# Other SBUF places and another order of sums for the last rows of x in a layer-scale kernel

## The chip, the cores and the metric

The kernel runs on one core of one Trainium2 chip. The metric is the device time of one execution in microseconds (us); lower is better.

## The reference

`x` and `y` are [1024, 16, 512] in bf16, `gamma` is [512] in bf16. The result is elementwise, with `gamma` spread over the first two dimensions:

```python
def reference(x, y, gamma):
    return x + gamma * y
```

Flattened, there are 16,384 rows of 512 elements. Each of the three large tensors (x, y and the output) has 16.78 MB.

## The kernel before

The 16,384 rows are divided over the 128 partitions of SBUF: each partition holds 128 rows of 512 elements, 1 KB per row and partition. "Row r" below means row r of every partition, so one row stands for 128 KB of data. `BLOCKS = [4, 64, 60]` says how the rows lie in DRAM: rows 0 to 4, 4 to 68 and 68 to 128 are three blocks, and within a block the rows of one partition are contiguous. A transfer of rows 4 to 68 is therefore 128 contiguous stretches of 65,536 bytes, one for each partition; one of rows 68 to 128 is 128 stretches of 61,440 bytes, and one of rows 68 to 120 is 128 stretches of 53,248 bytes.

The whole of y stays in SBUF (`y_sb`, 128 rows). The product and the sum are both written over it, and the output is stored from it. For x there are only 76 places (`x_sb`, 76 rows), so that the last rows of x are loaded over rows that have already been used. The lists at the top of the file set everything:

- `SP` is the sequence of loads that SyncE (SP) issues. `('x', 68, 120, 16)` loads rows 68 to 120 of x into the places from 16 on. `ACT` is the sequence that ScalarE issues: gamma, then three stores, of rows 4 to 68, 0 to 4 and 68 to 128.
- `PIECES = [16, 52, 52, 8]` cuts the 128 rows into the pieces that VectorE works on: piece 0 is rows 0 to 16, piece 1 rows 16 to 68, piece 2 rows 68 to 120, piece 3 rows 120 to 128.
- `DVE` is VectorE's sequence. `('m', c)` multiplies piece c of y by gamma in place (L181), `('a', c)` adds x to it (L190).
- `HOLD` and `AHEAD`: SP waits before its third load until rows 0 to 4 of y are in.
- `RELEASE`: the stores wait until the load of rows 68 to 120 of x has landed. TensorE waits for it and then raises two semaphores, `s_go` for ScalarE (L159) and `s_rel` for VectorE (L160).

Ahead of each load of x, `frees(w)` finds the pieces whose sums read the places that the load will write over, and SP waits until that many sums are done (semaphore `s_add`, which every sum raises by one; L36 is the helper for other waits). SP's queue is in order: the wait ahead of one load also holds back those behind it. In the kernel before, the load of rows 68 to 120 goes over places 16 to 68, which piece 1 reads, and piece 1 is summed first; so SP waits for one sum, and then issues this load and the load of rows 120 to 128 (into places 68 to 76, which nothing used before) one directly after the other (L133).

gamma is spread over the partitions by one matmul with a row of ones (L153) and a copy out of PSUM (L155). At the end SP waits for all stores.

Of the kernel before, what the change touches and what calls it, by code (L numbers as in the profile page):

```python
# [5 lines left out]

BLOCKS = [4, 64, 60]

PIECES = [16, 52, 52, 8]


SP = [
# [2 lines left out]
    ('x', 0, 4, 0),  # L15
    ('x', 4, 68, 4),
    ('y', 68, 128),
    ('x', 68, 120, 16),
    ('x', 120, 128, 68),
]  # L20
ACT = [('g',), ('s', 4, 68), ('s', 0, 4), ('s', 68, 128)]

# [1 line left out]

HOLD, AHEAD = ('y', 0, 4), (2, 0)

RELEASE = ('x', 68, 120, 16)

DVE = [('m', 0), ('m', 1), ('a', 1), ('a', 0), ('m', 2), ('m', 3), ('a', 2), ('a', 3)]
MULT, ADD = mybir.AluOpType.mult, mybir.AluOpType.add  # L30


def _take(sem, n, eng):


    return eng.wait_ge(sem, n).then_inc(sem, -n)  # L36


def kernel(
# [18 lines left out]
    rows = N // P  # L58
    n = len(PIECES)
    assert sum(PIECES) == rows  # L60
    starts = [sum(PIECES[:c]) for c in range(n + 1)]
    dt = xf.dtype
# [27 lines left out]
    s_add, s_go, s_rel, s_end, s_out = sem("s_add"), sem("s_go"), sem("s_rel"), sem("s_end"), sem("s_out")  # L90
    added = [a for kind, *a in DVE if kind == "a"]
    order = {a[0]: k for k, a in enumerate(added)}

    def meets(a, b, c, d):
        return a < d and c < b
# [4 lines left out]
    def x_at(row):  # L100
        return next(w[3] + row - w[1] for w in x_loads if w[1] <= row < w[2])
# [55 lines left out]

    _take(s_load[RELEASE], 16, nc.tensor)
    nc.tensor.sem_inc(s_go, 1)  # L159
# [4 lines left out]
    def need(loads, c):  # L164
        for w in loads:
            if w not in landed and meets(starts[c], starts[c + 1], w[1], w[2]):
                if w == RELEASE:
                    _take(s_rel, 1, nc.vector)
                elif w == HOLD:
                    _take(s_held[nc.vector], 1, nc.vector)  # L170
                else:
                    _take(s_load[w], 16, nc.vector)
                landed.add(w)

    for kind, *args in DVE:
        c = args[0]
        yt = y_sb[:, starts[c] : starts[c + 1], :]
        if kind == "m":
            need(y_loads, c)
            g = gamma_sb[:, None, :].to_broadcast([P, PIECES[c], D])  # L180
            nc.vector.tensor_tensor(out=yt, in0=yt, in1=g, op=MULT).then_inc(s_dve, 1)  # L181
            open_mults += 1
        else:
# [4 lines left out]
            at = x_at(starts[c])  # L188
            xt = x_sb[:, at : at + PIECES[c], :]
            nc.vector.tensor_tensor(out=yt, in0=xt, in1=yt, op=ADD).then_inc(s_add, 1)  # L190
# [44 lines left out]
```

## Time and profile before

| | |
|---|---|
| time, median of 7 executions | 120.51 us (120.27 to 120.65) |
| time of the profiled execution | 120.31 us |
| its span in the trace | 119.0 us (118.99 before rounding) |
| moved by DMA | 50.33 MB, 423 GB/s over the span |
| VectorE busy | 69.9 us, 59% |
| TensorE (PE) busy | 0.6 us |

The span is the part of an execution that the trace covers; 1.32 us of the profiled time lie outside it. Times inside the trace count from the start of the span. "From issue to landing" is the time from the instruction that issues a transfer to the moment when all of it has arrived. Where the text speaks of windows, a row gives the window, its length, the busy time of each engine in it with the number of instructions, the TensorE clock, the busy time of the 16 DMA engines as a share of 16 engines over that window, and the rate. In that view a DMA engine's transfer of one stretch counts whole in the window in which it starts, so the share of a short window can be far above 1. From such a row follow the number of stretches that start in it (rate times length, divided by the bytes of a stretch) and their mean duration (share times 16 times length, divided by that number).

### The profile page before, as it was taken

What the parts mean: (1) busy time and instruction counts of PE and PEld (TensorE: products, weight loads), DVE (VectorE), ACT (ScalarE), POOL (GpSimd) and SP (SyncE); (2) the same over time, 40 slices, a digit from 0 to 9 for tenths busy, and PEclk for the clock granted to TensorE, in tenths of its full rate; (3) what the DMA queues carried; (4) which work ended last, traced back from release to release, by engine and by line L of the source; (5) the groups of instructions that cost most, each with busy time, mean ns of one, the idle gap of its engine ahead of it and who ended that gap; (6) DMA issues with size and microseconds to landing.
All of it is one profiled execution on the core that took longest, in us unless ns stands there. A gap on an engine that the chain in (4) does not pass through costs nothing. (4 is left out here: it accounts for less than half of the span.)

```text
span 119.0 us, 89 instructions
## 1 busy us (share of the span) xinstructions
PE 0.6 (0%) x1; PEld 0.1 (0%) x1; DVE 69.9 (59%) x10; POOL 0.2 (0%) x4
## 2 busy tenths in 40 slices
PE   0001000000000000000000000000000000000000
PEld 0000000000000000000000000000000000000000
DVE  0002000399999839999999999989999800000000
POOL 0000000000000000000000000000000000000000
DMA  9888998988898879779869797998898889798790
GB/s 529 352 353 352 529 529 352 529 352 352 352 683 375 352 330 661 330 330 640 351 286 555 304 555 304 386 606 352 352 683 375 352 352 507 330 640 351 330 640 21
DMA packets 1442, 50.33 MB, mean 423 GB/s; under 512 B 161, under 2 KB 162, under 8 KB 546
## 3 DMA queue, kind: packets, MB, share of 16 engines
q1 hardware_dynamic: 1008, 33.55, 65.8%
q10 hardware_dynamic: 434, 16.78, 32.7%
HBM read 33.56 MB, written 16.78 MB: 423 GB/s over the span
## 5 line engine op out<-in xcount | busy, mean ns | idle before, releaser
L181 DVE TENSOR_TENSOR y_sb<-y_sb,gamma_sb 128x26624 bf16<-128x26624 bf16 (+2 forms) x4 | 34.6, 8686 | 11.0 <-DVEq L36 11.0
L190 DVE TENSOR_TENSOR y_sb<-x_sb,y_sb 128x26624 bf16<-128x26624 bf16 (+2 forms) x4 | 34.6, 8688 | 2.8 <-DVEq L36 2.8
L155 DVE CAST gamma_sb<-gamma_ps 128x512 bf16<-128x512 f32 x1 | 0.7, 691 | 9.0 <-DVEq L36 9.0
L147 DVE MEMSET ones_row<- 1x128 bf16 x1 | 0.2, 165 | 2.0 <-PEq L52 2.0
L153 PE MATMUL gamma_ps<-gamma_row,ones_row 1*128 1x512 bf16 x1 | 0.6, 577 | 10.4 <-PEq L36 10.4
L153 PEld LDWEIGHTS gamma_ps<-gamma_row,ones_row 1*128 1x128 bf16 x1 | 0.1, 99 | 10.4 <-issue 10.4
L219 POOL MEMSET const-bfloat16-1.0<- 128x1 bf16 x1 | 0.1, 102 | 0.0
L219 POOL MEMSET const-uint8-127<- 128x1 uint8 x1 | 0.1, 102 | 0.0
L219 POOL MEMSET const-float32-1.0<- 128x1 f32 x1 | 0.1, 99 | 0.0
L219 POOL MEMSET const-float32-0.0<- 128x1 f32 x1 | 0.1, 98 | 0.2 <-issue 0.2
## 6 DMA issues: line engine op xcount, KB each, us to landing
y_sb<-in_y_dram SPq DMA_DIRECT2D x1, 7680.0 KB, 57.0
out_dram<-y_sb ACTq DMA_DIRECT2D x1, 7680.0 KB, 24.2
x_sb<-in_x_dram SPq DMA_DIRECT2D x1, 6656.0 KB, 20.2
x_sb<-in_x_dram SPq DMA_DIRECT2D x1, 1024.0 KB, 22.3
y_sb<-in_y_dram SPq DMA_DIRECT2D x1, 512.0 KB, 3.3
x_sb<-in_x_dram SPq DMA_DIRECT2D x1, 512.0 KB, 20.3
out_dram<-y_sb ACTq DMA_DIRECT2D x1, 512.0 KB, 22.3
y_sb<-in_y_dram SPq DMA_DIRECT2D x1, 22.3
```

The costliest lines, as they stand in the source:

```text
L147: nc.vector.memset(ones_row, 1.0).then_inc(s_ones, 1)
L153: nc.tensor.matmul(gamma_ps, ones_row, gamma_row, start=True, stop=True).then_inc(s_ps, 1)
L155: nc.vector.tensor_copy(out=gamma_sb, in_=gamma_ps).then_inc(s_dve, 1)
L181: nc.vector.tensor_tensor(out=yt, in0=yt, in1=g, op=MULT).then_inc(s_dve, 1)
L190: nc.vector.tensor_tensor(out=yt, in0=xt, in1=yt, op=ADD).then_inc(s_add, 1)
L219: nc = _bacc.Bacc("TRN2", target_bir_lowering=False, num_devices=1)
```

## The change

The lists at the top of the file change, the code below them does not. Rows 0 to 68 are cut into three pieces instead of two, so there are five pieces: rows 0 to 8, 8 to 24, 24 to 68, 68 to 120 and 120 to 128. The load of rows 68 to 120 of x goes into places 24 to 76 instead of 16 to 68, and the load of rows 120 to 128 into places 0 to 8 instead of 68 to 76; `x_sb` keeps its 76 places. VectorE first sums rows 24 to 68, then rows 0 to 8, then rows 8 to 24. What `frees` answers changes with it: the load of rows 68 to 120 waits for one sum, which is now that of 44 rows, and the load of rows 120 to 128 waits for a second sum, that of rows 0 to 8.

```diff
-PIECES = [16, 52, 52, 8]
+PIECES = [8, 16, 44, 52, 8]
...
     ('y', 68, 128),
-    ('x', 68, 120, 16),
-    ('x', 120, 128, 68),
+    ('x', 68, 120, 24),
+    ('x', 120, 128, 0),
 ]
...
-RELEASE = ('x', 68, 120, 16)
-
-DVE = [('m', 0), ('m', 1), ('a', 1), ('a', 0), ('m', 2), ('m', 3), ('a', 2), ('a', 3)]
+RELEASE = ('x', 68, 120, 24)
+
+DVE = [('m', 0), ('m', 1), ('m', 2), ('a', 2), ('a', 0), ('a', 1), ('m', 3), ('m', 4), ('a', 3), ('a', 4)]
```

The stores still need the sums of their own rows: three sums instead of two for rows 4 to 68, five instead of four for the last store. Their order and sizes, and those of the loads, stay as they are.

## Prediction

> **What bounds the kernel now.** I read the page's load lines first, then VectorE's timeline, the waits of SP's queue, the DMA issues, and last narrow windows around the moment at which one load hands over to the next.
>
> ```profile
> DMA  9888998988898879779869797998898889798790
> ...
> q1 hardware_dynamic: 1008, 33.55, 65.8%
> q10 hardware_dynamic: 434, 16.78, 32.7%
> HBM read 33.56 MB, written 16.78 MB: 423 GB/s over the span
> ```
>
> The DMA engines are busy from end to end. 50.33 MB at 423 GB/s is the whole span. A stretch of 61,440 bytes takes 2.267 us on one engine (last row of the window table below: 1.42 x 16 x 0.10), which is 27.1 GB/s, or 434 GB/s for sixteen; at that pace 50.33 MB take 116.1 us. The first transfer starts at 1.0 us, and SP sees the last landing about 0.37 us after it ends. So some 1.5 us of the 119.0 are left for everything else. VectorE, busy 69.9 us, is not the bound, as its timeline shows:
>
> ```profile
> 22.83 18.36 DVE L181 TENSOR_TENSOR y_sb<-y_sb,gamma_sb 128x8192 bf16<-128x8192 bf16 x2 [11.02 <-DVEq L36]
> 43.58 18.36 DVE L190 TENSOR_TENSOR y_sb<-x_sb,y_sb 128x26624 bf16<-128x26624 bf16 x2 [2.39 <-DVEq L36]
> 57.63 0.81 SPq L133 DMA_DIRECT2D x_sb<-in_x_dram  x2
> 61.85 16.22 DVE L181 TENSOR_TENSOR y_sb<-y_sb,gamma_sb 128x26624 bf16<-128x26624 bf16 x2
> 78.20 16.89 ACTq L139 DMA_DIRECT2D out_dram<-y_sb  x3
> 78.49 16.23 DVE L190 TENSOR_TENSOR y_sb<-x_sb,y_sb 128x26624 bf16<-128x26624 bf16 x2 [0.41 <-DVEq L36]
> ```
>
> VectorE waits 2.39 us for x before its first sum at 43.58. That sum ends at 57.60, and at 57.63 SP issues the two last loads. The next two lines say that SP had waited for that sum, and how long the loads took:
>
> ```profile
> SPq L133 <- DVE y_sb L190: 52.7, 1, 52.7
> ```
>
> ```profile
> y_sb<-in_y_dram SPq DMA_DIRECT2D x1, 7680.0 KB, 57.0
> ...
> x_sb<-in_x_dram SPq DMA_DIRECT2D x1, 6656.0 KB, 20.2
> x_sb<-in_x_dram SPq DMA_DIRECT2D x1, 1024.0 KB, 22.3
> ```
>
> The load of y's last 60 rows, issued at 4.50, lands 57.0 us later, at 61.5. So when SP issues x's next load at 57.63, the engines still have some 3 us of y to move. Seen this way the issue is not late, and the change would buy nothing. The windows around the handover say more:
>
> ```profile
> 42.50:42.60 0.10, 0.00 (x0) 0.00 (x0) 0.00 (x0) 0.00 (x0) 1.00 5.70 2458
> 60.66:60.73 0.07, 0.00 (x0) 0.00 (x0) 0.07 (x1) 0.00 (x0) 1.00 8.49 3043
> 60.73:61.20 0.47, 0.00 (x0) 0.00 (x0) 0.47 (x1) 0.00 (x0) 1.00 3.15 1360
> 62.65:63.15 0.50, 0.00 (x0) 0.00 (x0) 0.50 (x1) 0.00 (x0) 1.00 3.69 1597
> 63.15:63.70 0.55, 0.00 (x0) 0.00 (x0) 0.55 (x1) 0.00 (x0) 1.00 0.00 0
> 63.70:63.80 0.10, 0.00 (x0) 0.00 (x0) 0.10 (x1) 0.00 (x0) 1.00 1.23 532
> 115.60:116.00 0.40, 0.00 (x0) 0.00 (x0) 0.00 (x0) 0.00 (x0) 1.00 5.33 2304
> 116.00:116.30 0.30, 0.00 (x0) 0.00 (x0) 0.00 (x0) 0.00 (x0) 1.00 0.00 0
> 116.30:116.40 0.10, 0.00 (x0) 0.00 (x0) 0.00 (x0) 0.00 (x0) 1.00 1.42 614
> ```
>
> The first row is the handover from x's rows 4 to 68 to y's rows 68 to 128, whose load had been issued 38 us before. Four stretches start in it (2458 x 0.10 / 61,440 bytes), mean 2.28 us: the normal 2.267. The next two rows are the handover to the load issued at 57.63. The twelve engines that reach it after 60.73 need 1.97 us for 53,248 bytes, but the four that reach it before 60.73 need 2.38 us on average (8.49 x 16 x 0.07 / 4), together 1.6 us too long. The transfer records show where this lies: 3.02 us instead of 1.97 on one engine, 0.36 and 0.18 us too long on two others, nothing on any later one. The rows from 62.65 on show the result: fifteen engines start their second stretch by 63.15, none in the next 0.55 us, one at 63.75. An engine that was among the first four is now the last by 0.62 us. It never recovers, because every engine has the same bytes still to move: in the last three rows fifteen engines start their last stretch before 116.00, none for 0.3 us, and one at 116.35. That engine ends at 118.62, the one before it at 118.16. So the end of the span is one engine's delay of 1.05 us, of which 0.45 shows.
>
> That only the first to arrive were delayed is how it looks when something of the new load (its descriptors, or the first data) is not ready yet. The latest engine got going at about 60.73 + 1.05 = 61.78, that is 4.15 us after the issue.
>
> **The change part by part.**
>
> The sums that decide the issue. The groups by shape give VectorE's price per row:
>
> ```profile
> L190 DVE TENSOR_TENSOR y_sb<-x_sb,y_sb 128x26624 bf16<-128x26624 bf16 x2 | 28.1, 14026 | 2.8 <-DVEq L36 2.8
> L190 DVE TENSOR_TENSOR y_sb<-x_sb,y_sb 128x8192 bf16<-128x8192 bf16 x1 | 4.4, 4418 | 0.0
> L190 DVE TENSOR_TENSOR y_sb<-x_sb,y_sb 128x4096 bf16<-128x4096 bf16 x1 | 2.3, 2284 | 0.0
> ```
>
> From 4,096 to 26,624 elements is 11.74 us for 44 rows of 512. So the new sum of 44 rows costs 11.74 + 0.15 (what is left of the 2.28) = 11.89 us, against 14.03. It still starts at 43.58: the three products ahead of it take 2.28 + 4.42 + 11.89 = 18.59 us, against 18.44 for two, which ends by 41.4, inside the wait for x. Without that cover of 2.2 us the extra product would cost about 0.1. The sum ends at 55.47, so SP issues x's rows 68 to 120 at 55.49, 2.14 us sooner. The lead over the first engine's arrival at 60.69 grows from 3.06 to 5.20 us. The slowest engine needed 4.15, so 1.05 us are to spare, and its delay goes: -1.05 us on that engine. Late next is the engine that ends at 118.16: -0.45 us on the span.
>
> The load of rows 120 to 128. It gets a wait of its own, for the sum of rows 0 to 8, which ends 2.2 us later, at 57.7. It is issued at about 57.7 instead of 58.0. Nothing stands behind it in SP's queue but the final waits, and its bytes come after those of rows 68 to 120, from 76.4 on: the lead is 18.7 us. Cost: nothing; it would have to be some 14 us later to matter.
>
> The release. Rows 68 to 120 land at 57.63 + 20.2 = 77.85 now; without the late engine, 0.5 us sooner. The stores (78.20 in the timeline) follow 0.35 us behind that landing, so at 77.7. The loads of rows 120 to 128 keep the engines busy until 79.0 to 79.5, which covers that issue as it does now. Store and load may then overlap a little on an engine; the bytes are the same, and I put this at 0. By the trace, where stores start at 79.07 with 2.48 instead of 2.42 us on the engines that come first, its bounds are -0.1 and +0.1 us.
>
> VectorE afterwards. One product and one sum more, and each adds about 0.07 us to the pace of the chain (0.15 of fixed time, of which 0.08 overlaps the instruction before, as the starts in the timeline show: 14.03 + 4.42 = 18.45 for a line of 18.36). The products of the last 60 rows end at 78.14 instead of 78.07. The next sum starts at 78.49 now, held by the release; later by the products, at about 78.3. The last sum ends at 94.6 instead of 94.7. The last store's bytes have their turn at 99.76. Cost: nothing under a cover of 5 us; without it, 0.07 us.
>
> Here a rule of the Trainium skill speaks against the change. The page "DMA: Bandwidth & Descriptors", section "Latency and other measured facts", puts the first byte of a transfer issued from SP or ScalarE at about 0.6 us. By it a lead of 3.06 us hides the start five times over, the extra lead is worth 0.00 us, and the forecast would be 120.51. The row 60.66:60.73 disagrees for a queue whose engines are all busy: 4.15 us on the worst of sixteen. The trace's own cold start agrees with the rule more nearly (issued at 0.00, first stretch at 1.00). I go by the row, since it was measured at this very place. Its weakness is that it is one event in one execution.
>
> The sum: 118.99 - 0.45 = 118.54 us of span, 119.86 with the 1.32 outside it. The profiled execution (120.31) stands 0.20 below the median of 120.51; applied to the median, 120.51 - 0.45 = 120.06. Executions above the profiled one may have had a longer or more unfortunate delay, in which case they gain more.
>
> **The rivals.**
>
> Same: the delay isn't tied to the lead. It could be a chance event of that execution, or belong to the first reads of rows 68 to 120 wherever they are issued. For it: only one load in the trace is issued late, and 3 us ought to suffice by the rule. Against it: that the three that were hit are all among the first four of sixteen would be 1 in 140 by chance, and no early load shows it. Time 120.51, 120.4 to 120.6. That the change doesn't move the issue at all can nearly be excluded: SP's wait is for one sum, and that sum is shorter.
>
> Slower: the delay is made by issuing any load while the engines are in their last stretch of y (58.4 to 61.1), when the generation of its descriptors gets in the way of theirs. Rows 120 to 128 are still issued at 57.7, so the delay stays and may fall on another engine. The engines arrive from 60.69 to 61.17. An engine delayed by 1.05 us that arrives at p ends at 118.62 + (p - 60.73); for the last one that is +0.44 us, 120.95. It is slower by over 0.24 us from p = 60.97 on, which is five of sixteen engines. For it: in the last stretch of y most transfers take 10 to 30 ns more than 2.267 us, and 65 on one. Against it: in the trace the late engines were spared.
>
> **How the numbers follow.** The delay goes: 0.62, at 120.06. Its own range is 119.8 to 120.25: at best 0.7 us is gained, if the median's extra 0.20 is the same delay on a later engine (the free engines ending between 117.9 and 118.16 set the floor), at worst half of it remains. Same: 0.22, at 120.51. Slower: 0.16, at 120.95. A measurement of this kernel can tell 0.2% (0.24 us) from no change, and the first case lies beyond that. The range of 119.75 to 120.65 takes in the first two and the small end of the third, and leaves out about 0.15.
>
> **What would show it.** Right: SP issues rows 68 to 120 at about 55.5; the stretches that start first at the handover near 60.7 take 1.97 us like the later ones; no engine starts its second stretch alone after 63.2; sixteen engines start their last stretch within about 0.5 us; ScalarE's first store is issued near 77.7. Wrong: an engine with a first stretch of over 2.5 us is still there, or the last stretch still starts alone. In that case the time has not moved, or has grown.

## The result and the profile after

The changed kernel takes 119.78 us (median of 12 executions, 119.70 to 120.02), the kernel before 120.45 us (median of 31, 119.88 to 120.76). The ratio is 0.9951, with a 95% interval of 0.9940 to 0.9962: 0.5% faster, some 0.6 us. The profiled span is 118.42 us, against 118.99.

The page of the changed kernel shows the same picture as before, full DMA engines over the whole span, a little denser:

```profile
DMA  9888998988899879979969696898899889798792
...
HBM read 33.56 MB, written 16.78 MB: 425 GB/s over the span
```

The timeline shows SP's two last loads (the line of 55.57), the first stores (77.63) and VectorE's groups:

```profile
43.65 18.43 DVE L190 TENSOR_TENSOR y_sb<-x_sb,y_sb 128x22528 bf16<-128x22528 bf16 x3 [2.29 <-DVEq L36]
55.57 2.53 SPq L133 DMA_DIRECT2D x_sb<-in_x_dram  x2
62.00 16.22 DVE L181 TENSOR_TENSOR y_sb<-y_sb,gamma_sb 128x26624 bf16<-128x26624 bf16 x2
77.63 17.33 ACTq L139 DMA_DIRECT2D out_dram<-y_sb  x3
78.36 16.23 DVE L190 TENSOR_TENSOR y_sb<-x_sb,y_sb 128x26624 bf16<-128x26624 bf16 x2
```

SP issues rows 68 to 120 at 55.57, 2.06 us sooner than before. The second issue of that line is at 57.77. The DMA issues of the two loads, with the time to landing in the last column:

```profile
x_sb<-in_x_dram SPq DMA_DIRECT2D x1, 6656.0 KB, 21.7
x_sb<-in_x_dram SPq DMA_DIRECT2D x1, 1024.0 KB, 22.0
```

Rows 68 to 120 now need 21.7 us instead of 20.2, so of 2.06 us of earlier issue 1.5 are spent waiting in the queue, and the landing is 0.56 us sooner (77.28 instead of 77.85). What the earlier issue brings is seen in the windows, read as in the prediction:

```profile
60.55:60.73 0.18, 0.00 (x0) 0.00 (x0) 0.18 (x1) 0.00 (x0) 1.00 4.80 2071
60.73:61.20 0.47, 0.00 (x0) 0.00 (x0) 0.47 (x1) 0.00 (x0) 1.00 2.36 1020
62.50:63.15 0.65, 0.00 (x0) 0.00 (x0) 0.65 (x1) 0.00 (x0) 1.00 3.02 1311
63.15:63.70 0.55, 0.00 (x0) 0.00 (x0) 0.55 (x1) 0.00 (x0) 1.00 0.00 0
115.10:115.75 0.65, 0.00 (x0) 0.00 (x0) 0.00 (x0) 0.00 (x0) 1.00 3.49 1512
115.75:116.40 0.65, 0.00 (x0) 0.00 (x0) 0.00 (x0) 0.00 (x0) 1.00 0.00 0
```

Seven stretches start in the first row and nine in the second, with a mean of 1.97 us in both: nobody is delayed at the handover. All sixteen engines start their second stretch by 63.15, and all sixteen their last one by 115.75. Before, one engine did the first at 63.75 and the second at 116.35.

### The profile page after: what moved, and what is told of

It is laid out like the page before. It is cut to its first block, busy times and chain, and to the rows that moved or that the text cites. A ratio compares the mean times of both kernels' runs of the same rounds, so it can differ in the third digit from the quotient of the medians.

```text
span 118.4 us, 91 instructions
## 1 busy us (share of the span) xinstructions
PE 0.6 (0%) x1; PEld 0.1 (0%) x1; DVE 70.1 (59%) x12; POOL 0.2 (0%) x4
## 5 line engine op out<-in xcount | busy, mean ns | idle before, releaser
L181 DVE TENSOR_TENSOR y_sb<-y_sb,gamma_sb 128x4096 bf16<-128x4096 bf16 (+3 forms) x5 | 34.6, 6980 | 11.1 <-DVEq L36 11.1
L190 DVE TENSOR_TENSOR y_sb<-x_sb,y_sb 128x4096 bf16<-128x4096 bf16 (+3 forms) x5 | 34.7, 6981 | 2.4 <-DVEq L36 2.3
## 6 DMA issues: line engine op xcount, KB each, us to landing
x_sb<-in_x_dram SPq DMA_DIRECT2D x1, 6656.0 KB, 21.7
```

## Experiments

The lead is the time from SP's issue of rows 68 to 120 of x to the moment when the first engine has finished y and turns to them. The theory: where the lead is short, some engines are delayed at the handover, and the kernel ends with the most delayed one. The rivals: chance; the new places and pieces; two loads issued close together; a fixed need of about 4 us; the last stretch of y.

**The kernel before once more.** No edit; a second profile of it.

> The kernel before, unchanged, for a second profile of it. Lead theory: first stretches of 53,248 bytes near 60.7 that take over 2.2 us are there again, perhaps on other engines and of another size; span 118.6 to 119.2. Rival (a chance event of the one profiled execution): none, span 118.4 to 118.6.

It took 120.78 us, just above the range given for this kernel in the section on the result; the span was 119.46. The windows of this run:

```profile
60.70:61.25 0.55, 0.00 (x0) 0.00 (x0) 0.55 (x1) 0.00 (x0) 1.00 3.52 1452
61.25:62.05 0.80, 0.00 (x0) 0.00 (x0) 0.80 (x2) 0.00 (x0) 1.00 0.00 0
62.05:62.10 0.05, 0.00 (x0) 0.00 (x0) 0.05 (x1) 0.00 (x0) 1.00 2.65 1065
116.00:116.35 0.35, 0.00 (x0) 0.00 (x0) 0.00 (x0) 0.00 (x0) 1.00 6.09 2633
116.35:116.80 0.45, 0.00 (x0) 0.00 (x0) 0.00 (x0) 0.00 (x0) 1.00 0.00 0
116.80:116.85 0.05, 0.00 (x0) 0.00 (x0) 0.00 (x0) 0.00 (x0) 1.00 2.83 1229
```

Fifteen engines start on x by 61.25, with a mean of 2.06 us. The sixteenth starts at 62.07 and needs 2.12 us. In the last three rows the same gap has come through to the end: one engine starts its last stretch 0.6 us after all others. So the delay is no chance event of one execution, but which engine it hits, and how hard, changes. In the first profile it was one of the earliest to arrive. Here it is one that was through with y at 61.01 or 61.06, later than most; it then stood idle for about 1.0 us, and more of the delay shows. It ends at 119.09, the latest engine of the first profile at 118.62. The span, 119.46, is outside the 118.6 to 119.2 that I had expected.

**The order of the sums undone.**

```diff
-DVE = [('m', 0), ('m', 1), ('m', 2), ('a', 2), ('a', 0), ('a', 1), ('m', 3), ('m', 4), ('a', 3), ('a', 4)]
+DVE = [('m', 0), ('m', 1), ('m', 2), ('a', 0), ('a', 2), ('a', 1), ('m', 3), ('m', 4), ('a', 3), ('a', 4)]
```

(against the changed kernel)

> The changed kernel with one part undone: VectorE sums rows 0 to 8 ahead of rows 24 to 68. Five pieces and the new places stay. The sum that SP waits for ends at about 57.7 again, both loads are issued one after the other at 57.7 and 58.1, the lead over the first engine's arrival falls to about 3 us. Lead theory (the delay comes from issuing too shortly before the engines run out of y): the delay is back, a first stretch of over 2.3 us near 60.7, time 120.3 to 120.5, ratio 0.999 to 1.001. Rival (the new places or the smaller pieces are what helps): no delay, 119.8, ratio 0.995.

Measured: 120.5 us, ratio to before 1.0000 (0.9987 to 1.0014). The whole gain is gone. Its timeline and its windows:

```profile
57.70 0.80 SPq L133 DMA_DIRECT2D x_sb<-in_x_dram  x2
```

```profile
60.70:60.81 0.11, 0.00 (x0) 0.00 (x0) 0.11 (x1) 0.00 (x0) 1.00 4.54 1937
60.81:61.00 0.19, 0.00 (x0) 0.00 (x0) 0.19 (x1) 0.00 (x0) 1.00 6.70 2522
61.00:61.20 0.20, 0.00 (x0) 0.00 (x0) 0.20 (x1) 0.00 (x0) 1.00 1.90 799
```

The middle row holds nine stretches with a mean of 2.26 us; the four before and the three after it are near normal (2.00 and 2.03). The new places and the five pieces alone bring nothing. Note that the delayed engines are not the first to arrive here.

**The second wait alone.**

```diff
-    ('x', 120, 128, 68),
+    ('x', 120, 128, 0),
```

(against the kernel before)

> The kernel before with one part of the change alone: rows 120 to 128 of x go to places 0 to 8, so that their load waits for a second sum and is issued at about 62 instead of 58.0. Rows 68 to 120 are issued at 57.63 as before. Lead theory: the delay stays, 120.3 to 120.5, ratio 0.999 to 1.001. Rival (the delay comes from two loads issued one right behind the other while the engines are in their last stretch of y): the delay is gone, 119.8, ratio 0.995.

Measured: 120.48 us, ratio 1.0008 (0.9994 to 1.0022). The last load is issued at 62.0, apart from the other, and there are still delays; in the windows of this run the four stretches of the middle row have a mean of 2.23 us, and the longest of them takes 2.60 us by the transfer records:

```profile
60.70:60.74 0.04, 0.00 (x0) 0.00 (x0) 0.04 (x1) 0.00 (x0) 1.00 9.27 3994
60.74:60.81 0.07, 0.00 (x0) 0.00 (x0) 0.07 (x1) 0.00 (x0) 1.00 7.96 3043
60.81:61.20 0.39, 0.00 (x0) 0.00 (x0) 0.39 (x1) 0.00 (x0) 1.00 2.85 1229
```

So the delay does not need two loads issued close together.

**More and less lead.** The number of rows in the first sum sets when SP may issue. Each of three kernels has the order and number of pieces of the kernel before, with other sizes; the two with 48 and 50 rows also put rows 120 to 128 into places 0 to 8.

48 rows:

```diff
-PIECES = [16, 52, 52, 8]
+PIECES = [20, 48, 52, 8]
...
-    ('x', 68, 120, 16),
-    ('x', 120, 128, 68),
+    ('x', 68, 120, 20),
+    ('x', 120, 128, 0),
...
-RELEASE = ('x', 68, 120, 16)
+RELEASE = ('x', 68, 120, 20)
```

> A lead between the two: the first sum has 48 rows (rows 20 to 68), the load of rows 68 to 120 goes to places 20 to 72 and is issued at about 56.6, a lead of 4.1 us; four pieces; rows 120 to 128 go to places 0 to 8 after the sum of 20 rows. Lead theory with a need of up to 4.15 us on the slowest engine: the delay all but gone, 119.8 to 120.1, ratio 0.995 to 0.998. If the need is only that the load arrives before the engines begin their last stretch of y (58.3): gone altogether, 119.8. Rival (chance or the order of sums): 120.45.

50 rows:

```diff
-PIECES = [16, 52, 52, 8]
+PIECES = [18, 50, 52, 8]
...
-    ('x', 68, 120, 16),
-    ('x', 120, 128, 68),
+    ('x', 68, 120, 18),
+    ('x', 120, 128, 0),
...
-RELEASE = ('x', 68, 120, 16)
+RELEASE = ('x', 68, 120, 18)
```

> The lead between 3.06 and 4.1 us: the first sum has 50 rows (18 to 68), the load of rows 68 to 120 goes to places 18 to 70 and is issued at about 57.1, a lead of 3.6 us; four pieces; rows 120 to 128 go to places 0 to 8. A fixed need of up to 4.15 us: half of the gain, 120.0 to 120.25. The need to be there before the last stretch of y begins (58.3, that is 1.2 us after the issue): nearly all of it, 119.8 to 120.0.

60 rows:

```diff
-PIECES = [16, 52, 52, 8]
+PIECES = [8, 60, 52, 8]
```

> A shorter lead: the first sum has 60 rows (rows 8 to 68), everything else as before, so both loads are issued at about 59.8, only 0.9 us ahead of the first engine's arrival. If every load needs up to 4.15 us from issue to its start on the slowest engine: that engine starts at 63.9, 3.2 us after its turn, and the time is 122 to 123. If the need is about 1 us, as at the kernel's start, and the delay of before comes from arriving in the middle of the last stretch: all engines start at 60.8 to 61.2, the delays are below 0.5 us, and the time is 119.9 to 120.5.

| kernel | issue, us | lead, us | longest loss of an engine at the handover, us | time, us | ratio to before (95%) |
|---|---|---|---|---|---|
| 60 rows | 59.86 | 0.8 | at least 1.2 | 120.92 | 1.0054 (1.0032 to 1.0076) |
| before, 52 rows | 57.63 | 3.06 | 1.05 | 120.45 | 1 |
| 52 rows, second wait alone | 57.68 | 3.03 | 0.63 | 120.48 | 1.0008 (0.9994 to 1.0022) |
| 50 rows | 57.28 | 3.48 | 0.13 | 119.82 | 0.9957 (0.9943 to 0.9971) |
| 48 rows | 56.59 | 4.06 | 0.01 | 119.83 | 0.9953 (0.9940 to 0.9966) |
| changed, 44 rows | 55.57 | 5.02 | 0.00 | 119.78 | 0.9951 (0.9940 to 0.9962) |

The losses are from the transfer records: the time by which an engine's first stretch is longer than 1.966 us, with the idle time ahead of it. Each is from one profiled execution, while the time is a median. With 60 rows several engines stood idle at once and the records do not name the engine, so that only a lower bound can be given there. The windows of the handover with 48 rows, then with 50, then with 60 rows:

```profile
60.60:60.73 0.13, 0.00 (x0) 0.00 (x0) 0.13 (x1) 0.00 (x0) 1.00 5.71 2458
60.73:61.20 0.47, 0.00 (x0) 0.00 (x0) 0.47 (x1) 0.00 (x0) 1.00 2.63 1133
```

```profile
60.70:60.89 0.19, 0.00 (x0) 0.00 (x0) 0.19 (x1) 0.00 (x0) 1.00 3.91 1682
60.89:61.30 0.41, 0.00 (x0) 0.00 (x0) 0.41 (x1) 0.00 (x0) 1.00 3.03 1299
```

```profile
60.80:61.10 0.30, 0.00 (x0) 0.00 (x0) 0.30 (x1) 0.00 (x0) 1.00 5.17 1598
61.10:62.00 0.90, 0.00 (x0) 0.00 (x0) 0.90 (x2) 0.00 (x0) 1.00 1.15 414
```

With 48 rows six stretches and then ten have a mean of 1.98 us, and with 50 rows 1.98 and 1.99. With 60 rows it is 2.76 us for the nine of the first row and 2.37 for the seven of the second: every engine waits. Two things follow. First, the gain comes in full between leads of 3.03 and 3.48 us: the row with the second wait alone and the row with 50 rows differ in two rows of the first sum and in little else. Two rows fewer, together with the second wait, would have brought it. Whether the longer lead would do it without the second wait is open: in the kernels with 44, 48 and 50 rows the two last loads of x are issued at least 2.2 us apart, and no run has a longer lead with both issued one directly after the other. Second, there is no fixed need of 4.15 us. With 60 rows, where the first engines had run out of work, the first stretch started 0.96 us after the issue and all engines got going 1.6 to 2.5 us after it (the start of a first stretch plus what it took too long), and the time is far from the 122 to 123 that a fixed need would give. It is also above the 119.9 to 120.5 of the other expectation, since I had put the delays at less than 0.5 us.

**Shorter stretches ahead of the handover.**

```diff
-    ('y', 68, 128),
+    ('y', 68, 98),
+    ('y', 98, 128),
```

(against the kernel before)

> The kernel before, except that y's rows 68 to 128 are loaded by two transfers of 30 rows, so that the stretches with which the engines finish y take 1.13 us instead of 2.27. The two loads of x are still issued at 57.6 and 58.0, the lead stays at about 3.1 us. If a load needs a fixed 4 us from its issue when the engines are busy: the delay stays, 120.3 to 120.5, ratio 0.999 to 1.001. If the need is that the load is there before an engine begins the last stretch ahead of it (that begins now at 59.5 instead of 58.4, 1.9 us after the issue): the delay is gone, 119.8 to 119.95, ratio 0.995 to 0.996.

Measured: 120.33 us, ratio 1.0000 (0.9983 to 1.0017). The windows of this run show seven stretches with a mean of 2.40 us and nine with 2.07:

```profile
60.85:61.00 0.15, 0.00 (x0) 0.00 (x0) 0.15 (x1) 0.00 (x0) 1.00 6.99 2485
61.00:61.40 0.40, 0.00 (x0) 0.00 (x0) 0.40 (x1) 0.00 (x0) 1.00 2.91 1198
```

I had come to suspect that a load must be there before an engine begins its last stretch of y. With stretches of half the length, and a lead of 3.1 us, the delays stay, so that idea falls.

**The same moment of issue, a later turn.**

```diff
-    ('x', 68, 120, 16),
     ('x', 120, 128, 68),
+    ('x', 68, 120, 16),
```

(against the kernel before)

> The kernel before, with x's two last loads in the other order: rows 120 to 128, whose places are free, are loaded directly behind y, and give the engines 2.5 us more work ahead of rows 68 to 120. Those are issued at 57.6 as before, after the same sum; only their turn moves from 60.7 to 63.2, so that the lead is 5.5 us. Lead theory: all first stretches of 53,248 bytes take 1.97 us. Rival (the moment of issue, 57.6, with what VectorE and the engines do then): delays of over 0.2 us remain. The time says little here: the stores are released by the landing of rows 68 to 120, which is now the last load, with nothing behind it to cover their start; about 0.9 us of idle engines, less the delay that goes: 120.7 to 121.2.

Rows 68 to 120 are issued at 57.71, as before, but their turn is 2.4 us later. The windows of this run, the first two at the handover and the last two at the start of the stores:

```profile
63.10:63.30 0.20, 0.00 (x0) 0.00 (x0) 0.20 (x1) 0.00 (x0) 1.00 4.80 2069
63.30:63.60 0.30, 0.00 (x0) 0.00 (x0) 0.30 (x1) 0.00 (x0) 1.00 3.70 1598
79.40:80.95 1.55, 0.00 (x0) 0.00 (x0) 0.54 (x1) 0.00 (x0) 1.00 0.00 0
80.95:81.15 0.20, 0.00 (x0) 0.00 (x0) 0.20 (x1) 0.00 (x0) 1.00 12.39 5243
```

The second row holds nine stretches of 53,248 bytes with a mean of 1.97 us. The first holds seven, and beside them five of the small ones of rows 120 to 128 (8,192 bytes, 0.309 us each by the transfer records): 2069 x 0.20 is 7 x 53.2 + 5 x 8.2 KB, and 4.80 x 16 x 0.20 less 5 x 0.309 leaves 1.97 us for each of the seven. Nobody is delayed. The kernel with the second wait alone issues at the same moment (57.68), also apart from the other load, and has delays; its turn comes at 60.7. So the lead decides, and not the moment of issue or what VectorE does at that moment. The time is 121.74 us, ratio 1.0105 (1.0087 to 1.0122), a miss: I had expected 120.7 to 121.2. In the third row no transfer starts for 1.55 us, and in the fourth the stores begin. The engines stand idle for about 2.0 us on average, since nothing covers the way from the last stretch of x over its landing and the release to the issue of the stores (80.12) and their first stretch (80.99). I had counted only the last leg of that way. In the other kernels the load of rows 120 to 128 covers it.

**From a queue that is idle.**

```diff
 SP = [
...
-    ('x', 68, 120, 16),
-    ('x', 120, 128, 68),
 ]
-ACT = [('g',), ('s', 4, 68), ('s', 0, 4), ('s', 68, 128)]
+ACT = [('g',), ('x', 68, 120, 16), ('x', 120, 128, 68), ('s', 4, 68), ('s', 0, 4), ('s', 68, 128)]
```

(against the kernel before)

> The kernel before, with x's two last loads issued by ScalarE, whose own queue is idle then, instead of SP, after the same sum (57.6 and 58.0). The lead stays at 3.1 us. If the long need (over 3 us) comes from standing behind other work in the same queue: the engines find the new load within about 1 us, as they do for the first store (issued 78.20, first turn 79.07), take it in turns with the rest of y, and no stretch of x is delayed; y lands up to 2 us later, which the products of VectorE follow, and the time is 119.7 to 120.1. If the need is the same on any queue while the engines are busy: delays of 0.2 to 1 us near 60.7 as before, 120.3 to 120.6.

Measured: 120.47 us, ratio 1.0007 (0.9994 to 1.0019). The delays stay: the sixteen first stretches, all in the window below, have a mean of 2.08 us, and one engine loses 0.74 us by the transfer records. No engine takes a stretch of x before it is through with y.

```profile
60.60:61.30 0.70, 0.00 (x0) 0.00 (x0) 0.70 (x1) 0.00 (x0) 1.00 2.97 1217
```

The timeline of ScalarE shows something else:

```profile
57.67 3.71 ACTq L131 DMA_DIRECT2D x_sb<-in_x_dram  x2
```

Issuing these two loads takes 3.71 us, of which the second issue has 3.31. On SP the same pair took 0.81 us. Having a queue to itself did not make the load ready sooner.

**Still more lead, and the same thought at the start.** Two kernels against the changed one. In the first, x's rows 68 to 90 are loaded over the rows of a still shorter first sum, issued at 49.74; in the second the first loads take 8 rows instead of 4.

```diff
-PIECES = [8, 16, 44, 52, 8]
+PIECES = [8, 16, 22, 22, 52, 8]
...
-    ('x', 68, 120, 24),
+    ('x', 68, 90, 24),
+    ('x', 90, 120, 46),
...
-RELEASE = ('x', 68, 120, 24)
+RELEASE = ('x', 90, 120, 46)
...
-DVE = [('m', 0), ('m', 1), ('m', 2), ('a', 2), ('a', 0), ('a', 1), ('m', 3), ('m', 4), ('a', 3), ('a', 4)]
+DVE = [('m', 0), ('m', 1), ('m', 2), ('m', 3), ('a', 2), ('a', 3), ('a', 0), ('a', 1), ('m', 4), ('m', 5), ('a', 4), ('a', 5)]
```

> The changed kernel with more lead: the first sum is cut to 22 rows (24 to 46), rows 68 to 90 of x are loaded over them, issued at about 49.7, and rows 90 to 120 over rows 46 to 68 after the next sum, at about 55.6. Six pieces. Lead theory: a lead of 5.2 us was enough, so nothing more is gained, 119.75 to 119.9, ratio 0.995. Rival (more lead still helps, since engines drift apart elsewhere for the same reason): below 119.6.

```diff
-BLOCKS = [4, 64, 60]
+BLOCKS = [8, 60, 60]
...
-    ('y', 0, 4),
-    ('y', 4, 68),
-    ('x', 0, 4, 0),
-    ('x', 4, 68, 4),
+    ('y', 0, 8),
+    ('y', 8, 68),
+    ('x', 0, 8, 0),
+    ('x', 8, 68, 8),
...
-ACT = [('g',), ('s', 4, 68), ('s', 0, 4), ('s', 68, 128)]
+ACT = [('g',), ('s', 8, 68), ('s', 0, 8), ('s', 68, 128)]
...
-HOLD, AHEAD = ('y', 0, 4), (2, 0)
+HOLD, AHEAD = ('y', 0, 8), (2, 0)
```

> The changed kernel, with the same thought applied to its start: the first loads of y and x take 8 rows instead of 4 (blocks of 8, 60 and 60 rows), so that the second load of y, issued at 0.4, is reached at about 3.6 instead of 2.3, a lead of 3.2 instead of 1.9 us. In the changed kernel its first stretches take 0.1 to 0.45 us too long on most engines. Lead theory: part of that goes, 119.5 to 119.75. Rival (these first stretches are slow because everything starts at once): 119.75 to 119.9.

Measured: 119.90 us, ratio 0.9962 (0.9949 to 0.9975), and 119.92 us, ratio 0.9952 (0.9937 to 0.9967). The first is within what was expected of the lead theory; the second is a miss, just above both expected ranges. More lead brings nothing beyond the changed kernel. At the start the long first stretches of y's second load do go: every one takes 2.267 us. But by the transfer records the engines reach that load 1.77 us later, where four rows more are worth 1.2 us (8 x (0.309 - 0.159)), so the loss has moved into the first load. None of these kernels is faster than the changed one.

## Why the prediction was right, and where its sizes were off

The direction, the place and the mechanism were right, and the measured 119.78 us lies in the range of 119.75 to 120.65, but at its very low end: below the 120.06 of the text, and just below the 119.8 to 120.25 that I had given to this case. By its steps:

The issue. 55.49 was worked out, 55.57 measured; 57.77 for the second load against 57.7. The extra product lay in the wait for x, as the step said.

The delay goes. It does: the first stretches are all normal, and the runs with the order undone and with the same moment but a later turn show that the lead does it.

What comes next. Here a term was mis-sized. I let the span end with the engine that ended at 118.16 before, -0.45 us. But the last engine now ends at 117.97, 0.65 us sooner than the last one before, of which the span shows 0.57. By the transfer records the mean end of the sixteen engines moved too, from 118.04 to 117.67. The other engines had also been slowed, a little at a time. All 128 stretches of 53,248 bytes together took 3.2 us longer than 1.966 us each, only half of that in the first ones; now it is 0.02 us, that is 0.2 us per engine. The stretches of the stores lost 1.6 us in total, now 0.07, another 0.1 per engine. That the longer lead removed these small losses is not shown. With the second wait alone, at the same short lead, the later stretches of x lost 0.13 us in total and the stores 0.01; with 50 rows, where the gain is there in full, the later stretches still lost 0.57. What the runs tie to the lead are the delays of the first stretches. And the second profile of the kernel before shows what else my sum lacked: a delay on an engine that arrives late counts in full. I had kept that case for the low end of the range.

The lead needed. "The slowest engine needed 4.15" was read from one engine and is no threshold: 3.1 us was still too short and 3.5 us enough. The reading that only the first to arrive are hit was wrong as well: with the order undone it was those in the middle, in the second profile a late one. The conclusion held by its margin and not by these two readings: 5 us are above either figure.

The release and VectorE. Stores issued at 77.63 (worked out: 77.7), the next sum at 78.36 (78.3), the last store at 94.62, 4.7 us ahead of its turn at 99.32; no stretch of it is delayed.

The rule of the Trainium skill. By "DMA: Bandwidth & Descriptors", section "Latency and other measured facts", 0.6 us to the first byte would have made the change worth nothing. The runs side with the trace's row at the handover, 60.66:60.73: a lead of 3.0 to 3.1 us, with the engines busy, left delays in every one of the six profiles that had it, and 3.48 us left one of 0.13. With the first four engines idle the first stretch started 0.96 us after the issue, nearer to the page's figure. The measurement decides.

The rival "slower", that issuing any load during the last stretch of y does the harm, is ruled out by the changed kernel: its last load is issued at 57.77, where that rival put it, and nobody is delayed.

Open is what takes the 3 us and more. It may be the descriptors of the new load, which come late while the engines are full, or the first data. The slow second issue on ScalarE (3.31 us), and that of the stores (1.53 us in the kernel before, 0.45 in the changed one), hint at the first; no run separates the two.

## What to carry to other kernels

Where DMA is the bound, don't judge a load's issue by whether the queue still holds work when it comes: look at the first stretches after the handover, engine by engine, because one delayed engine stays late to the end. Here a lead of 3.0 us was too short and one of 3.5 us enough, with the next load issued apart from it, and it was bought by cutting the piece that frees the space and summing it first; more lead brought nothing. Keep something in the queue behind the transfer that releases the next phase: without it the engines stood idle for about 2.0 us here.

## What the runs showed of the hardware

A load issued 3.0 to 3.1 us before its turn, with all sixteen engines busy, found some engines without it: in six profiles the longest delay was 0.6 to about 1.2 us, on engines at different places in the order of arrival. At 3.48 us there was one of 0.13 us, at 4.06 and more none above 0.02. Where four engines had run dry the first stretch started 0.96 us after the issue. An idle second queue did not take the delays away, and the second of two issues in a row took 3.31 us there (0.44 on SP). The scatter of the times goes the same way: 0.9 us for the kernel before (119.88 to 120.76), 0.3 for the changed one (119.70 to 120.02); with 22 executions each, 1.06 us with the order undone and 0.32 with the load in two parts.
